# Moving and widening the reduced piece of a streaming grouped convolution: from one piece of 64 columns in slot 23 to pieces of 72 and 4 columns in slot 10

## The chip, the core and the metric

The kernel runs on one core of one Trainium2 chip. The metric is device time in microseconds (us) of one execution. The kernel before has a median of 483.09 us over 4 runs (480.42 to 483.26). One execution was taken with the hardware profiler; it took 481.27 us, and its span, from the first to the last instruction, is 479.5 us.

## What is computed

A grouped convolution with a 1 x 1 window, so nothing but a small matrix product for each pixel and group:

```
H = W = 512;  G = 4;  Cg = 48;  C = 192          # x, out: (1, 512, 512, 192) bf16
out[b, h, w, g, :] = x[b, h, w, g, :] @ w[0, 0, g]    # w: (1, 1, 4, 48, 48)
```

There are 262144 pixels of 192 channels (384 bytes), 100.66 MB in and 100.66 MB out. The arithmetic is small; every byte crosses the DMA engines once in and once out.

## The kernel before

**Tiling.** A "column" is one pixel on each of the 128 partitions, so 128 pixels. A *piece* is a block of columns that one load brings to the ring `ring` and whose result goes out in one or more stores. A *full* piece gives every one of the 128 rows the same number of columns (mostly 80), and its load is a single DMA on SyncE's queue, 128 rows of 80 x 384 = 30720 bytes. The pieces fill numbered *slots* of 80 columns; slot n lies in part n % 3 of the ring (240 columns), and its load waits until TensorE has read slot n - 3 (`freed`, which returns a count of pairs for the semaphore `t_done`).

**The reduced piece.** One piece isn't full. `PARTIAL` lists five blocks of rows, 120 rows in all: rows 16 to 19 and 48 to 51 are left out. Two blocks of 16 rows go by SyncE's queue (loads) and ScalarE's queue (stores), the other three (44, 12 and 32 rows) by GpSimd's. Each block is cut into an outer dimension of units of 4 rows (4, 4, 11, 3 and 8 units), and two tiny "filler" DMAs of 5 rows stand before GpSimd's first and second block. `plan_pieces` (line 73) puts this piece of 64 columns into slot 23; the eight rows left out thus hold 64 columns fewer of the image than the others: 1988 columns against 2052. GpSimd waits for `freed` too, issues its three loads (line 241), waits for `go_sem` from ScalarE, and issues its three stores (line 247).

**Order of pieces.** Slot 0 is split into 8, 24 and 48 columns; slots 1 to 22 are full; 23 is the reduced piece; 24 is full with 80; 25 has the 68 columns that remain. `plan_stores` (line 95) gives each piece one store, except near the end: full pieces with fewer than 240 columns behind them are stored 40 columns at a time, and the last piece, if its size is 68, in parts of 24, 20, 16 and 8 (`LAST_PARTS`). Stores take their place in turn in the output ring `oring` of 280 columns; one that meets the end of the ring is cut in two.

**Compute.** Four columns are a *group* (513 in all), two groups a *pair* (257). For a group TensorE does 6 transposes (line 291) to PSUM; VectorE copies a pair to SBUF (line 349); TensorE does 6 matmuls (line 311) with the block weights; ScalarE copies the group from PSUM to `oring` (line 386), first waiting until the store that last used those columns has landed. ScalarE also issues the stores (line 367), each one group after its last column.

**Program order on TensorE.** `step(pair)` issues the transposes of the next pair and the matmuls of this one. `loop_span` finds the run of full 80-column slots after slot 0, and a loop (`Fori`) of 30 pairs repeats 7 times over slots 1 to 22. Pairs 0 to 9 and the last 37 are written out. In the program there are so 10 + 30 + 37 = 77 pairs of instructions. The other engines' programs are written out in full.

Of the kernel before, what the change touches and what calls it, by code (L numbers as in the profile page):

```python
# [24 lines left out]
BIG = 80  # L25
SLOTS = 3
RCOLS = SLOTS * BIG
# [5 lines left out]
NXP = 4  # L33
NXS = 3
NOB = 4
NTOK = 6
# [3 lines left out]
PARTIAL = (  # L40
    ("sync", 0, 16, 4), ("sync", 32, 16, 4),
    ("pool", 52, 44, 11), ("pool", 20, 12, 3), ("pool", 96, 32, 8),
)
PARTIAL_COLS = 64
PARTIAL_SLOT = 23

FILL_ROWS = 5
FILL_BEFORE = (2, 3)
# [22 lines left out]


def plan_pieces(npix):
    few = PARTIAL_COLS * sum(b[2] for b in PARTIAL)
    partial = npix >= few + 128 * BIG * PARTIAL_SLOT
    cols = (npix - few * partial) // 128
    assert cols % 4 == 0
    head = list(HEAD) if cols >= sum(HEAD) else []
    mid = cols - sum(head)
    slots = [[(BIG, FULL)]] * (mid // BIG) + ([[(mid % BIG, FULL)]] if mid % BIG else [])  # L80
    if head:
        slots.insert(0, [(s, FULL) for s in head])
    if partial:
        slots.insert(PARTIAL_SLOT, [(PARTIAL_COLS, PARTIAL)])
    pieces, g, pix = [], 0, 0
    for n, parts in enumerate(slots):
        c = n % SLOTS * BIG
        for s, blocks in parts:
            pieces.append(Piece(len(pieces), n, c, g, s, blocks, pix))
            c, g, pix = c + s, pieces[-1].g1, pieces[-1].pix_end  # L90
    assert pix == npix
    return pieces
# [21 lines left out]
    return stores  # L114


def loop_span(pieces, ng):

    body = RCOLS // 4
    a = next((p.g0 for p in pieces if p.slot == 1), ng)  # L120
    b = a
    for p in pieces:
        if p.slot >= 1 and p.g0 == b and p.full and p.size == BIG:
            b = p.g1

    rounds = max(0, (b - a - 2) // body)
    return a, body, rounds


def bass_standalone__grouped__vision_kernel(nc, x, w, out):  # L130
# [3 lines left out]
    assert npix % 512 == 0, "the pixel count must be a multiple of 512"  # L134

    pieces = plan_pieces(npix)
    stores = plan_stores(pieces)
    piece_of = {g: p for p in pieces for g in range(p.g0, p.g1)}
    store_of = {g: s for s in stores for g in range(s.g0, s.g1)}
    NG = pieces[-1].g1  # L140
    NP = (NG + 1) // 2
    LA, LB, LR = loop_span(pieces, NG)
    assert LA % 2 == 0 and LB % (2 * NXS) == 0 and LB % (2 * NTOK) == 0 and LB % NXP == 0

    xf = x.rearrange("b h w c -> (b h w) c")
    of = out.rearrange("b h w c -> (b h w) c")
# [2 lines left out]
    def groups(pair):  # L149
        return range(2 * pair, min(2 * pair + 2, NG))  # L150
# [14 lines left out]
    ld_key = {}  # L165
    for p in pieces:
        part = sum(1 for q in pieces if q.slot == p.slot and q.i < p.i)
        for n in range(len(p.blocks)):
            ld_key[p.i, n] = (p.slot % SLOTS, part) if p.full else ("partial", n)
    partial = [p for p in pieces if not p.full]  # L170

    with ExitStack() as es:
        block = es.enter_context(nc.Block())
# [26 lines left out]
        def columns(g):  # L200
            p = piece_of[g]
            at = p.at + 4 * (g - p.g0)
            return ring[:, at * C:(at + 4) * C]
# [6 lines left out]
        def freed(p):  # L210

            last = [q for q in pieces if q.slot == p.slot - SLOTS]
            return last[-1].g1 // 2 if last else 0

        @block.gpsimd
        def _(gp):
# [20 lines left out]
            for p in partial:  # L237
                gp.wait_ge(t_done, freed(p))
                for n, dram, sbuf in transfers(xf, ring, p.at, p, 0, p.size, ("pool",)):
                    filler(n)  # L240
                    gp.dma_start(sbuf, dram).then_inc(ld_sem[ld_key[p.i, n]], 16)  # L241
                gp.wait_ge(go_sem, 1)
                for i, s in enumerate(stores):
                    if s.piece is p:
                        for n, dram, sbuf in transfers(of, oring, s.at, p, s.c0, s.c1, ("pool",)):
                            filler(n)
                            gp.dma_start(dram, sbuf).then_inc(st_sem[i][n], 16)  # L247
# [3 lines left out]
        @block.sync  # L251
        def _(sp):
            sp.dma_start(w_sb[:], wv).then_inc(w_sem, 16)  # L253
            seen = 0
            for p in pieces:
                if freed(p) > seen:
                    seen = freed(p)
                    sp.wait_ge(t_done, seen)
                for n, dram, sbuf in transfers(xf, ring, p.at, p, 0, p.size, ("sync",)):
                    sp.dma_start(sbuf, dram).then_inc(ld_sem[ld_key[p.i, n]], 16)  # L260

        @block.tensor
        def _(pe):

            def build_weights():
                pe.wait_ge(e_sem, 1)
                pe.wait_ge(w_sem, 16)
                last = None
                for (tc, r, g, c0_) in WBLOCKS:
                    s0 = ESHIFT - r  # L270
                    col = WOFF[tc] + c0_
                    last = pe.matmul(o_ps[:, NOB - 1, col:col + CG], lhsT=esel[:, s0:s0 + 128],  # L272
                                     rhs=w_sb[:, g, :], start=True, stop=True, skip_group_check=True)
                last.then_inc(wb_sem, 1)

            def transposes(pair):
                todo = []
                for g in groups(pair):
                    p = piece_of[g]
                    if g % 2 and pair:  # L280
                        pe.wait_ge(e_done[(pair - 1) % NTOK], 1)
                    if g == p.g0:
                        keys = [ld_key[p.i, n] for n in range(len(p.blocks))]
                        for key in keys:
                            pe.wait_ge(ld_sem[key], 16)
                        todo += keys if p.full else []
                    xg = columns(g)
                    for ul in range(2):
                        for tc in range(3):
                            j = ul * 3 + tc  # L290
                            last = pe.transpose(xT_ps[:, g % NXP, j * 128:(j + 1) * 128],  # L291
                                                xg[:, j * 128:(j + 1) * 128], ident[:])
                            if todo and 0 < j < 5:
                                last.then_inc(ld_sem[todo.pop(0)], -16)
                assert not todo
                last.then_inc(t_done, 1)

            def matmuls(pair):
                if pair + 1 == NP or len(groups(pair + 1)) < 2:
                    pe.wait_ge(e_done[pair % NTOK], 1)  # L300
                for g in groups(pair):
                    xs = xT_sb[pair % NXS][:, g % 2 * 2 * UC:(g % 2 + 1) * 2 * UC]
                    if g >= 2:
                        pe.wait_ge(fa_done[(g - 2) % (2 * NTOK)], 1)
                    last = None
                    for ul in range(2):
                        v = 2 * g + ul
                        for tc in range(3):
                            j = ul * 3 + tc
                            c0_, c1_ = COLR[tc]  # L310
                            last = pe.matmul(o_ps[:, v % NOB, c0_:c1_], lhsT=xs[:, j * 128:(j + 1) * 128],  # L311
                                             rhs=wt[:, WOFF[tc]:WOFF[tc] + (c1_ - c0_)],
                                             start=(tc == 0), stop=(tc == 2), skip_group_check=True)
                            if j == 2 and g >= 2:
                                last.then_inc(fa_done[(g - 2) % (2 * NTOK)], -1)
                            if j == 1 and g % 2 == 0:
                                last.then_inc(e_done[pair % NTOK], -1)
                    last.then_inc(mm_done, 1)

            def step(pair):  # L320
                if pair + 1 < NP:
                    transposes(pair + 1)
                matmuls(pair)

            build_weights()
            pe.wait_ge(id_sem, 1)
            transposes(0)
            pe.wait_ge(wc_sem, 1)
            first = LA // 2 if LR > 1 else NP
            for pair in range(first):  # L330
                step(pair)
            if LR > 1:
                with pe.Fori(0, LR):
                    for pair in range(first, first + LB // 2):
                        step(pair)
                for pair in range(first + LR * LB // 2, NP):
                    step(pair)

        @block.vector
        def _(dve):  # L340
# [80 lines left out]
```

## Time and profile before

| what | value |
|---|---|
| median of 4 runs | 483.09 us (480.42 to 483.26) |
| the profiled execution, and its span | 481.27 us, 479.5 us |
| TensorE busy, weight loads busy | 430.9 us (90%), 390.3 us (81%) |
| ScalarE busy | 389.2 us (81%) |
| VectorE busy, GpSimd busy | 246.4 us (51%), 7.0 us (1%) |
| moved by DMA | 201.65 MB, mean 421 GB/s |
| granted TensorE clock | 0.974 |

How to read it: "busy" is the time in which an engine executes; TensorE's matmuls are pipelined, so its busy share isn't a share of its peak. A DMA is cut into packets, one for each row here; 16 DMA engines serve them, each taking one packet at a time from the queues in turn. The trace keeps start, duration, size and queue of every packet, and the time of every semaphore increment; a DMA's semaphore gets its increments as the engines finish their shares, so the sixteen times of one DMA tell how far the engines are apart. Times within the span are counted from its first instruction.

### The profile page before, as it was taken

The page shows a single profiled execution, that of the slowest core. Times are in us where ns is not written, and L with a number is a line of the kernel's source. Part 1 is how long each engine was busy: PE and PEld are TensorE (multiplying, and loading weights), DVE is VectorE, ACT ScalarE, POOL GpSimd, SP SyncE. Part 2 cuts the span into 40 slices and gives each one's busy share as a digit, 9 for nine tenths or more (in the row PEclk, how much of TensorE's full clock was granted, in tenths as well). Part 3 has the DMA queues.
Part 4 walks back from the last instruction along what each step waited for, and adds up shares of the span by engine and source line. Part 5 has one row for each costly group of instructions (what it writes and reads, how often), then busy time and mean ns, then how long its engine had stood idle before and what let it go on. Part 6 is the DMA issues. An engine that isn't in the chain of part 4 may idle for free.

```text
span 479.5 us, 13531 instructions
## 1 busy us (share of the span) xinstructions
PE 430.9 (90%) x6166; PEld 390.3 (81%) x6166; DVE 246.4 (51%) x258; ACT 389.2 (81%) x514; POOL 7.0 (1%) x18
## 2 busy tenths in 40 slices
PE   5999999999979989899899599999898987999894
PEld 4888888988868878788788498988787876888883
DVE  2555655555535545455355345555554543556452
ACT  2899999999958879689689479998797975988895
POOL 1000000000000000000000000000000020000200
PEclk9999999999989999899899889999999998999997
DMA  8999999999999999999999999999999999999986
GB/s 333 430 405 431 437 425 434 424 431 437 431 438 424 441 418 438 425 436 425 419 437 431 439 423 436 425 438 423 431 431 441 428 422 422 404 426 422 430 370 261
DMA packets 9991, 201.65 MB, mean 421 GB/s; under 512 B 1664, under 2 KB 1664, under 8 KB 2432
## 3 DMA queue, kind: packets, MB, share of 16 engines
q10 hardware_dynamic: 5224, 98.50, 48.2%
q1 hardware_dynamic: 4136, 98.52, 48.2%
q0 software_dynamic: 608, 4.33, 2.1%
q8 instruction: 14, 0.23, 0.2%
q14 instruction: 9, 0.07, 0.0%
HBM read 100.68 MB, written 100.66 MB: 420 GB/s over the span
## 4 chain that ended last, share of the span: by engine, by line
PE 46%; DMA 41%; ACT 9%; another core or an unknown queue 1%; issue 1%; ACTq 1%; SPq 0%
DMA out_dram<-oring 39%; PE o_ps L311 27%; PE xT_ps L291 19%; ACT oring L386 9%; DMA ring<-in_x_dram 1%; ACTq L367 1%; SPq L260 0%; SPq L253 0%; ACTq L360 0%; ACTq L369 0%
## 5 line engine op out<-in xcount | busy, mean ns | idle before, releaser
L386 ACT CAST oring<-o_ps 128x768 bf16<-128x768 f32 x513 | 387.9, 801 | 85.2 <-PE o_ps L311 44.1
L349 DVE COPY xT_sb<-xT_ps 128x1536 bf16<-128x1536 bf16 x257 | 245.7, 956 | 222.0 <-PE xT_ps L291 222.0
L311 PE MATMUL o_ps<-wt,xT_sb 128*128 128x144 bf16 (+1 forms) x3078 | 290.1, 237 | 37.2 <-ACT oring L386 33.0
L311 PEld LDWEIGHTS o_ps<-wt,xT_sb 128*128 128x128 bf16 x3078 | 213.7, 99 | 74.6 <-ACT oring L386 66.3
L291 PE MATMUL xT_ps<-ident,ring 128*128 128x128 bf16 x3078 | 222.5, 223 | 3.1 <-DMA ring<-in_x_dram 3.1
L291 PEld LDWEIGHTS xT_ps<-ident,ring 128*128 128x128 bf16 x3078 | 190.2, 100 | 6.1 <-issue 3.5
L234 POOL DMA_DIRECT2D fill<-in_x_dram x4 | 2.4, 598 | 439.4 <-PE xT_ps L291 382.1
L272 PE MATMUL o_ps<-w_sb,esel 48*128 48x48 bf16 x10 | 0.6, 209 | 2.7 <-DMA w_sb<-in_w_dram 2.7
L272 PEld LDWEIGHTS o_ps<-w_sb,esel 48*128 48x128 bf16 x10 | 0.4, 110 | 2.7 <-POOL esel L220 2.7
L342 DVE CAST wt<-o_ps 128x480 bf16<-128x480 f32 x1 | 0.7, 657 | 3.3 <-PE o_ps L272 3.3
L386 ACT ACT_TABLE_LOAD x1 | 1.3, 1283 | 0.8 <-PEq L406 0.8
L241 POOL DMA_DIRECT2D ring<-in_x_dram x3 | 1.7, 564 | 0.0
L247 POOL DMA_DIRECT2D out_dram<-oring x3 | 1.7, 556 | 0.0
L220 POOL TENSOR_SCALAR_AFFINE_SELECT esel<-esel 48x272 bf16<-48x272 bf16 x1 | 0.4, 402 | 0.0
L217 POOL MEMSET esel<- 48x272 bf16 x1 | 0.3, 318 | 0.3 <-POOLq L406 0.3
L224 POOL TENSOR_SCALAR_AFFINE_SELECT ident<-ident 128x128 bf16<-128x128 bf16 x1 | 0.3, 282 | 0.0
L218 POOL MEMSET ident<- 128x128 bf16 x1 | 0.2, 198 | 0.0
L406 POOL MEMSET const-float32-0.0<- 128x1 f32 x1 | 0.1, 98 | 0.3 <-issue 0.3
L406 POOL MEMSET const-bfloat16-1.0<- 128x1 bf16 x1 | 0.1, 102 | 0.0
L406 POOL MEMSET const-uint8-127<- 128x1 uint8 x1 | 0.1, 102 | 0.0
L406 POOL MEMSET const-float32-1.0<- 128x1 f32 x1 | 0.1, 98 | 0.0
## 6 DMA issues: line engine op xcount, KB each, us to landing
ring<-in_x_dram SPq DMA_DIRECT2D x23, 3840.0 KB, 24.7
out_dram<-oring ACTq DMA_DIRECT2D x18, 3840.0 KB, 44.7
out_dram<-oring ACTq DMA_DIRECT2D x9, 1920.0 KB, 41.9
out_dram<-oring ACTq DMA_DIRECT2D x3, 1152.0 KB, 10.7
ring<-in_x_dram SPq DMA_DIRECT2D x1, 3264.0 KB, 25.3
ring<-in_x_dram SPq DMA_DIRECT2D x1, 2304.0 KB, 11.0
out_dram<-oring ACTq DMA_DIRECT2D x1, 2304.0 KB, 27.0
out_dram<-oring ACTq DMA_DIRECT2D x4, 384.0 KB, 9.4
```

The source lines that it names most:

```text
L220: gp.affine_select(out=esel[:], in_=esel[:], pattern=[[-1, ECOLS]], compare_op=AluOpType.is_equal, fill=0.0, base=ESHIFT, channel_multipli ...
L234: gp.dma_start(dst, src).then_inc(fill_sem[k], 16)
L241: gp.dma_start(sbuf, dram).then_inc(ld_sem[ld_key[p.i, n]], 16)
L247: gp.dma_start(dram, sbuf).then_inc(st_sem[i][n], 16)
L272: last = pe.matmul(o_ps[:, NOB - 1, col:col + CG], lhsT=esel[:, s0:s0 + 128], rhs=w_sb[:, g, :], start=True, stop=True, skip_group_check=True)
L291: last = pe.transpose(xT_ps[:, g % NXP, j * 128:(j + 1) * 128], xg[:, j * 128:(j + 1) * 128], ident[:])
L311: last = pe.matmul(o_ps[:, v % NOB, c0_:c1_], lhsT=xs[:, j * 128:(j + 1) * 128], rhs=wt[:, WOFF[tc]:WOFF[tc] + (c1_ - c0_)], start=(tc == ...
L342: dve.tensor_copy(wt[:], o_ps[:, NOB - 1, 0:WCOLS]).then_inc(wc_sem, 1)
L349: dve.tensor_copy(xT_sb[pair % NXS][:, 0:n * 2 * UC].rearrange("p (g c) -> p g c", g=n), xT_ps[:, b0:b0 + n, 0:2 * UC]).then_inc(e_done[pa ...
L367: act.dma_start(dram, sbuf).then_inc(st_sem[i][n], 16)
L386: act.copy(out_columns(g).rearrange("p (u c) -> p u c", u=2), o_ps[:, v % NOB:v % NOB + 2, 0:UC]).then_inc(fa_done[g % (2 * NTOK)] if g < ...
L406: nc = _bacc.Bacc("TRN2", target_bir_lowering=False, num_devices=1)
```

## The change

```diff
-PARTIAL_COLS = 64
-PARTIAL_SLOT = 23
+REST = (("sync", 0, 16, 4),)
+PARTIALS = ((72, PARTIAL), (4, REST))
+PARTIAL_SLOT = 10
...
 def plan_pieces(npix):
-    few = PARTIAL_COLS * sum(b[2] for b in PARTIAL)
+    few = sum(cols * sum(b[2] for b in blocks) for cols, blocks in PARTIALS)
...
-        slots.insert(PARTIAL_SLOT, [(PARTIAL_COLS, PARTIAL)])
+        slots.insert(PARTIAL_SLOT, list(PARTIALS))
...
-def loop_span(pieces, ng):
...
-    rounds = max(0, (b - a - 2) // body)
-    return a, body, rounds
+def loop_spans(pieces):
+
+    body, out, run = RCOLS // 4, [], []
+    for p in pieces + [None]:
+        if p and p.full and p.size == BIG:
+            run.append(p)
+            continue
+        if run:
+
+            first = max((run[0].g0 - 1) // 2, 1)
+            rounds = (run[-1].g1 - 2 * first - 2) // body
+            if rounds > 1:
+                out.append((first, body // 2, rounds))
+        run = []
+    return out
...
-            ld_key[p.i, n] = (p.slot % SLOTS, part) if p.full else ("partial", n)
-    partial = [p for p in pieces if not p.full]
+            ld_key[p.i, n] = (p.slot % SLOTS, part) if p.full else ("partial", part, n)
+    partial = [p for p in pieces if any(b[0] == "pool" for b in p.blocks)]
...
-            return last[-1].g1 // 2 if last else 0
+            return -(-last[-1].g1 // 2) if last else 0
...
-            first = LA // 2 if LR > 1 else NP
-            for pair in range(first):
+            pair = 0
+            for first, body, rounds in LOOPS:
+                for pair in range(pair, first):
+                    step(pair)
+                with pe.Fori(0, rounds):
+                    for pair in range(first, first + body):
+                        step(pair)
+                pair = first + rounds * body
+            for pair in range(pair, NP):
                 step(pair)
```

The reduced piece is 72 columns wide and lies in slot 10. A second piece of 4 columns on rows 0 to 15 alone (`REST`, four units of 4 rows on the SyncE and ScalarE queues) follows it in the same slot, so that the full pieces still have a multiple of 4 columns. Full pieces now hold 1980 columns, so the eight left-out rows hold 1980 columns of the image, rows 0 to 15 hold 1980 + 72 + 4 = 2056 and all other rows 1980 + 72 = 2052. There are 514 groups, still 257 pairs.

What follows in the plan: slots 1 to 9 are full, slot 10 is the reduced one, slots 11 to 24 are full, and slot 25 has 60 columns. As 60 isn't the sum of `LAST_PARTS`, the last piece is stored in parts of 40 and 20. TensorE has two loops: 3 rounds of 30 pairs from pair 9, and 4 rounds of 30 pairs from pair 109; written out are pairs 0 to 8, 99 to 108 and 229 to 256. In the program there are so 9 + 30 + 10 + 30 + 28 = 107 pairs.

More of the change, by code (lines that the diff above doesn't have):

```diff
@@ L114, in plan_stores @@
     return stores
-def loop_span(pieces, ng):
[L119 to L124, printed above, removed]
-    rounds = max(0, (b - a - 2) // body)
-    return a, body, rounds
+def loop_spans(pieces):
[11 more added lines that the diff above has]
+    return out
 def bass_standalone__grouped__vision_kernel(nc, x, w, out):
@@ L141, in bass_standalone__grouped__vision_kernel @@
     NP = (NG + 1) // 2
-    LA, LB, LR = loop_span(pieces, NG)
-    assert LA % 2 == 0 and LB % (2 * NXS) == 0 and LB % (2 * NTOK) == 0 and LB % NXP == 0
+    LOOPS = loop_spans(pieces)
+    assert all(RCOLS // 4 % n == 0 for n in (2 * NXS, 2 * NTOK, NXP))
     xf = x.rearrange("b h w c -> (b h w) c")
@@ L328, in _ @@
             pe.wait_ge(wc_sem, 1)
-            first = LA // 2 if LR > 1 else NP
-            for pair in range(first):
-                step(pair)
[L332 to L337, printed above, removed]
+            pair = 0
[7 more added lines that the diff above has]
+            for pair in range(pair, NP):
+                step(pair)
         @block.vector
```

## The prediction

> **What bounds the kernel now.** I read the slices of the span first, then the table of busy time by stretch, then the waits of a stretch, last the timeline of the end and the trace's packet records.
>
> ```profile
> ACT  2899999999958879689689479998797975988895
> DMA  8999999999999999999999999999999999999986
> ```
>
> ScalarE has holes all through the run, the DMA engines only at both ends. The stretches put numbers to it (columns: length, busy time of the five engines, clock, DMA share, GB/s):
>
> ```profile
> 0.00:5.00 5.00, 0.85 (x14) 0.77 (x15) 0.66 (x1) 1.28 (x1) 1.32 (x8) 1.00 0.55 186
> 5.00:145.00 140.00, 132.41 (x1897) 120.81 (x1896) 75.66 (x79) 117.44 (x156) 0.00 (x0) 0.99 1.01 430
> ...
> 240.00:345.00 105.00, 96.57 (x1396) 87.93 (x1394) 56.40 (x59) 87.38 (x116) 0.00 (x0) 0.97 1.01 433
> ...
> 460.00:479.50 19.50, 12.41 (x174) 10.72 (x174) 6.78 (x8) 12.88 (x17) 0.00 (x0) 0.88 0.72 295
> ```
>
> The share is 1.0 in every long stretch from 5 to 460 us, whatever the engines do. The idle time is at the start (5 x 0.45 = 2.3 us) and at the end (19.5 x 0.28 = 5.5 us). So it is a DMA kernel with a short end in which computing sets the pace for most of the DMA engines. Waits in between matter only through that end. From 240 to 405 us these are ScalarE's:
>
> ```profile
> ACT oring L386 <- DMA out_dram<-oring: 16.4, 5, 5.7
> ACT oring L386 <- PE o_ps L311: 11.2, 41, 1.3
> ```
>
> It waited 16.4 us in 5 waits for stores to land. Yet there was room on average: by the packet records 1593 columns were stored at 400 us and 1720 computed, 127 apart in a ring of 280. The increments of one store's semaphore show why: the store whose landing ended the wait of 401.8 us had its median increment at 385.5, the second-last at 390.5 and the last at 401.8. One engine lags 16 us. From packet to packet on one engine the next starts 4 ns before the last ends, so an engine can be followed: one takes 1.22 us for a store row of 30720 bytes and 1.15 for a load row where the others take 1.138 (+4.4% on both). From 417 to 464 us I can follow it without a gap, and no row of the reduced piece is on it: it is the engine that the piece spares. I call it the slow engine.
>
> The end, with the last two stores:
>
> ```profile
> 473.99 0.34 ACTq L367 DMA_DIRECT2D out_dram<-oring  x1
> 474.37 0.80 ACT L386 CAST oring<-o_ps 128x768 bf16<-128x768 f32 x1 [0.44 <-PE o_ps L311]
> 475.20 0.34 ACTq L367 DMA_DIRECT2D out_dram<-oring  x1
> ```
>
> The last copy ends at 475.2, the span at 479.5, 4.3 us later. For the last store but two (20 columns) the increments have their median at 473.8, the second-last at 474.8, the last at 476.3. Followed back from its last packet (478.7), the last engine has no gap down to 406 us, and it carried rows of the reduced piece, at the nominal 1.138: it isn't the slow engine. The second-last fits the slow one (464.0 plus its 16, 24, 24 and 20 columns). So at the end one ordinary engine is latest, the slow one 1 to 1.5 us before it, and most wait for computing.
>
> **The change part by part.** One column on an engine's 8 rows costs 8 x 1.138/80 = 0.114 us in each direction.
>
> *Columns.* The slow engine loses 8 columns: 8 x 2 x 0.114 x 1.044 = 1.9 us. The ordinary engines had 1988 + 64 and get 1980 + 72: the same 2052. Four of them also get the small piece's units, half an engine's rows: 4 x 2 x 0.057 = 0.46 us. The engine that ends last gets 0 or +0.46.
>
> *Place.* The slow engine's credit (72 columns, 17 us with its slowness) comes at some 150 to 230 us in place of 390 to 460. The store lag (median to last increment) was 10.2 us for the store that landed at 234; it turns into a lead and grows back by the end. ScalarE's waits behind that engine after 240 us (16.4 us) then mostly go. What is late next is the second-slowest (5 us behind at 385 to 390), and then the ring itself: at the first waits, around 140 us, 180 to 195 columns were computed and not stored against 127 later. So computing comes up to 50 columns (some 10 us) nearer to the loads, and I take 5 as what lasts to the end. For the DMA engines the middle is worth 0: they were never idle there.
>
> *Moved issues.* The piece's loads wait for slot 7 in place of slot 20. Before, GpSimd's three landed 16 to 37 us after issue (the last at 423.2), and TensorE began pair 230, which needs them, at 425.2, 40.8 us after the pairs whose end releases them. In the new place the same stretch, pair 80 to 100, runs from 145.9 to 182.5, 36.5 us, so a stall of some 2 us there is possible. Queued behind TensorE's wait are only its own transposes and matmuls, and ScalarE's copies wait for those; the DMA engines go on with stores (175 columns, 20 us, are then computed and not stored). Cost 0; without that cover, 2. The small piece's load adds one more wait to it, on a DMA issued before the next slot's. Rounding `freed` up delays the later slots' loads by one group's copy (0.8 us); they land 24.7 us after issue, with two slots of computing (33 us) in hand: 0. ScalarE's issues of the two four-unit blocks took 2.0 us at 441.9 and 1.8 us more went by before its next copy; this stood in the computing of the end and now stands in the middle, with a third block; there the same 20 us of stores cover it. TensorE lost 2.0 us there (a pair of 3.61 in place of 1.6): gain for the end of computing, 2.
>
> *TensorE's loops.* Back edges and exits show no gap: pairs 40, 70, 100 and 220 take 1.5 to 1.7 us like the rest. Written-out code is fetched:
>
> ```profile
> q8 instruction: 14, 0.23, 0.2%
> ```
>
> Fourteen packets of 16384 bytes for 77 pairs, 0.95 us each; 107 pairs make 20. Six more are 5.7 us over 16 engines, mean 0.4 (consecutive ones weren't on one engine); between 0 and 1 for the engine that ends last; I take the mean.
>
> *The end.* Group 514 adds one copy (0.80) and makes the last pair whole (VectorE 0.96 against 0.56): +1.2 us for computing. The last stores are 40 and 20 columns against 24, 20, 16 and 8. If computing sets the end: the 40 are issued four copies before the last copy's end (3.3 us), their data starts 1.4 us after issue (as at 473.99) and takes 4.6, the 20 another 2.3; with 0.9 to the span's end this is 5.8 us behind the last copy in place of 4.3. If the DMA queue sets it, coarse stores cost nothing.
>
> **The sum.** Computing: 475.2 + 1.2 - 2.0 - 5 = 469.4, and 5.8 later 475.2. The ordinary engine that ends last: 479.5 + 0.4 for fetches, less what its luck changes. It lost 2.9 us after 405 in five long packets (one of 2.16 us in place of 1.14, a fetch and its follower); with the middle place another engine may be last. Between nothing and the 2.5 us that lie between last and median increment, I take the half, 1.25; the small piece counts with 4 engines in 15, 0.1: 479.5 + 0.4 + 0.1 - 1.25 = 478.7. The later of the two sums counts: the DMA engines. The profiled execution had 1.8 us around its span (481.27) and lies 0.4% under the median, so I scale: 483.09 x 478.7/479.5 = **482.3**, a gain of 0.2%. Its own range is 477.4 (479.5 + 0.4 - 2.5) to 481.0 (a whole fetch and the small piece on the last engine), on the median's scale 481.0 to 484.6.
>
> *A rule against the change.* The slow engine took 1.22 us for a store row and carries no row of the reduced piece. The Trainium skill (DMA: Bandwidth & Descriptors, "Latency and other measured facts") says that engines 7 and 15 are usually the slower ones, its cause being uncertain, and the page's "The descriptor swizzle" gives the spared rows 16 to 19 and 48 to 51 to engine 4. By the rule the spared engine would be a wrong one and its 1.9 us worth 0; no record here numbers the engines, but the chain of packets shows the slow one spared, and the sum goes by the chain.
>
> **The rivals.**
>
> *The whole end closes (faster).* Computing is 5 us or more earlier and no engine is far behind: then the 5.5 us of mean idle time at the end fall to about 2.3 (0.9 from the last landing to the span's end and 1.4 of spread), with 0.4 more for fetches: 479.5 - 3.2 + 0.4 = 476.7, 480.3 on the median's scale; with all but the 0.9 gone and one cheap fetch, 475, 478.6. For it: ScalarE's 16.4 us. Against: the last engine had no gap to close.
>
> *Computing sets the end (slower).* One mechanism, in the last 60 columns: ScalarE's waits stay, because the ring of 280 columns or the second-slowest engine takes over from the slow one, and the two coarse stores lie bare behind a longer chain. Last copy at 475.2 + 1.2 = 476.4 with the 2 us lost again at late store waits, end 482.2, 485.8 on the median's scale. It decides when the last copy is later than 478.7 - 5.8 = 472.9. For it: the chain of waits is TensorE and ScalarE from 402 us on; the parts 24, 20, 16 and 8 no longer fit.
>
> *It relieves what isn't the limit.* The slow engine wasn't last, so sparing it more and earlier changes ScalarE's waits and not the time: 479.5 + 0.4 = 479.9, 483.5. That lies in the forecast's own range and is counted with it.
>
> **How the numbers follow.** A measurement of this kernel tells about 0.5% from no change (480.7 to 485.5). Forecast with the last rival 0.49, the faster 0.29, the slower 0.22; the chances are these. The forecast of 482.3 is the likeliest case. The range goes down to the faster rival's floor (478.6) less a little for luck in packets, 478.0, and up past the slower one with a fetch and a stall on the last engine (482.2 + 1 = 483.2, 486.8): 487.0.
>
> **What would show it.** Right: DMA share 1.0 from 5 us to 465 or later; 20 packets of instructions; from 240 us on, ScalarE's waits for stores well under 16 us and the last increment of each store within some 5 us of the median; the last copy before 473. The slower rival: last copy after 474 and a gap of about 6 us behind it. The faster one: mean idle time at the end under 3 us. Wrong altogether: stalls of TensorE on `ring` around 185 us that reach the end, or holes in the DMA row in the middle.

## The result, and the profile after

The changed kernel takes 482.94 us in the median (480.44 to 490.28, 42 runs), the kernel before on the same chip 482.35 us (63 runs). The ratio is 1.0033, with a 95% interval of 1.0018 to 1.0049: a loss of a third of a per cent, inside the range of the prediction and on the other side of no change than its forecast. Some executions of either kernel take over 1.5% longer than its fastest; the ratio leaves them out and the medians don't, so the ratio isn't the quotient of the two medians (1.0012). The profiled execution of the changed kernel took 484.69 us with a span of 482.9 us; it lies 1.75 us above the median of its kernel, so its last microseconds have to be read with care.

First the page of the changed kernel: ScalarE's and the DMA engines' slices, and the queue of instruction packets (packets, MB, share of 16 engines).

```profile
ACT  2999999999959971979973899888988877888880
DMA  8999999999999999999999999999999999999994
...
q8 instruction: 20, 0.33, 0.2%
```

The 20 packets are there. The DMA row has no hole in the middle, as in the kernel before; its last digit fell from 6 to 4. So more of the engines are idle at the end, not fewer. The timeline of the end shows that computing isn't why:

```profile
467.93 0.34 ACTq L373 DMA_DIRECT2D out_dram<-oring  x1
...
468.31 3.06 ACT L392 CAST oring<-o_ps 128x768 bf16<-128x768 f32 x4 [0.44 <-PE o_ps L316]
...
471.40 0.34 ACTq L373 DMA_DIRECT2D out_dram<-oring  x1
```

The last copy ends at 471.4, 3.8 us earlier than before (475.2). But the span ends 11.5 us behind it in place of 4.3. The last store's increments tell who is late: median 476.5, second-last 480.8, last 482.4 (before: 478.1, 478.2, 479.0). Most engines finished 1.6 us earlier than before and two finished 1.8 and 3.4 us later than the last one before.

ScalarE's waits for stores between 240 and 405 us, and the stand of TensorE behind the piece's loads:

```profile
ACT oring L392 <- DMA out_dram<-oring: 10.0, 2, 7.7
```

```profile
176.95 1.06 PE L316 MATMUL o_ps<-wt,xT_sb 128*128 128x144 bf16 x12
187.84 1.44 PE L296 MATMUL xT_ps<-ident,ring 128*128 128x128 bf16 x12 [9.84 <-DMA ring<-in_x_dram]
```

16.4 us in five waits became 10.0 in two, one of them 7.7. And TensorE stood 9.84 us before pair 100, the first that reads the reduced piece: GpSimd's three loads were issued from 145 us on and landed at 162.7, 178.6 and 187.7. This is the stall "around 185 us" that the prediction named as a sign of being wrong altogether; whether it reaches the end is asked below.

Last the view that points at the cause. The columns are those of the table by stretch: length, busy time of the five engines, clock, DMA share, GB/s.

```profile
200.00:220.20 20.20, 18.23 (x272) 16.45 (x268) 10.81 (x12) 16.95 (x23) 2.76 (x5) 1.00 1.00 428
220.20:224.40 4.20, 4.14 (x63) 3.74 (x62) 2.60 (x3) 3.87 (x7) 0.00 (x0) 1.00 0.91 388
224.40:240.00 15.60, 15.37 (x230) 13.85 (x228) 8.72 (x10) 14.09 (x20) 0.00 (x0) 1.00 1.03 438
```

In 4.2 us the share falls to 0.91 and the rate to 388 GB/s, while every computing engine is busy. In the kernel before the same stretch shows 1.03. The column is inexact in so short a stretch, so I counted packets: from 220.2 to 224.5 us exactly 15 of the 16 engines had one, and from 282.6 to 284.4 us again. One engine in sixteen makes 0.06 in a share and nothing in the tenths of the page. Followed from packet to packet, the idle one is the slow engine, the very one that the reduced piece is there to spare. SyncE's issue times say why it stood: it issued its next loads at 223.2 and at 283.3, and the two stretches end 1.4 and 1.1 us later with packets of these loads. So the engine had nothing else queued.

### The profile page after: what moved, and what is told of

It reads as the page before. It is cut to its first block, busy times and chain, and to the rows that moved or that the text cites. A ratio compares the mean times of both kernels' runs of the same rounds, so it can differ in the third digit from the quotient of the medians.

```text
span 482.9 us, 13571 instructions
## 1 busy us (share of the span) xinstructions
PE 430.0 (89%) x6178; PEld 388.4 (80%) x6178; DVE 246.8 (51%) x258; ACT 388.6 (80%) x515; POOL 7.0 (1%) x18
## 4 chain that ended last, share of the span: by engine, by line
PE 48%; DMA 38%; ACT 8%; ACTq 1%; issue 1%; POOL 1%; SPq 0%
DMA out_dram<-oring 28%; PE o_ps L316 28%; PE xT_ps L296 20%; DMA ring<-in_x_dram 10%; ACT oring L392 8%; ACTq L373 1%; POOL fill L239 0%; POOL ring L246 0%; POOL out_dram L252 0%; SPq L265 0%; SPq L258 0%; ACTq L366 0%; ACTq L375 0%
## 5 line engine op out<-in xcount | busy, mean ns | idle before, releaser
L296 PE MATMUL xT_ps<-ident,ring 128*128 128x128 bf16 x3084 | 221.5, 222 | 12.8 <-DMA ring<-in_x_dram 12.8
```

## The experiments

All ratios are to the kernel before on the same chip, with 95% intervals. Four theories were written down at first: **M**, the piece in the middle costs (GpSimd's loads come late there and the DMA engines lose time); **E**, the coarse last stores; **F**, the six more instruction packets, each of which lies on one engine; **C**, the prediction's own, that stores cover what happens in the middle. **I**, the idle slow engine, came only when M had been narrowed down, and was written down before the last two runs. In the code cuts below, `...` stands for what is left out.

### The parts of the change alone

Place alone: one piece of 64 columns as before, without the small piece and with the old last parts, in slot 10.

```diff
-PARTIALS = ((72, PARTIAL), (4, REST))
+PARTIALS = ((64, PARTIAL),)
```

> The place alone: the reduced piece keeps its 64 columns and moves from slot 23 to slot 10; the last piece keeps 68 columns and its fine parts; two TensorE loops, 107 pairs written out. Theory M (the middle costs: GpSimd's loads come some 10 us after TensorE wants them, computing stands, and the DMA packets of that stage get longer, by some 1 us per engine): as slow as the whole change, ratio 1.002 to 1.005, with TensorE waiting 5 to 10 us on the ring near 180 us. Theory E (the coarse last stores of 40 and 20 cost): 0.998 to 1.001. Theory F (six more packets of instructions cost, each on one engine): 1.001 to 1.004, as under M, with no wait needed.

Measured: 1.0035 (1.0000 to 1.0071). In its trace (488.74 us, where the median is 483.54) the last copy ends at 480.6 and the median increment of the last store is at 483.5, so there most engines were late, not one alone. Size alone, with the place of before:

```diff
-PARTIAL_SLOT = 10
+PARTIAL_SLOT = 23
```

> The size alone: 72 and 4 columns in slot 23 as before, the last piece 60 in parts of 40 and 20, one TensorE loop and 76 pairs written out. Theory M: 0.998 to 1.001 (no stall in the middle, the slow engine relieved by 1.9 us). Theory E: 1.002 to 1.005. Theory F: 0.999 to 1.001.

Measured: 1.0053 (1.0011 to 1.0095). The last copy of this kernel ends at 480.1, 4.9 us later than before, and the span 5.4 us behind it. And the changed kernel with finer last parts:

```diff
-LAST_PARTS = (24, 20, 16, 8)
+LAST_PARTS = (24, 16, 12, 8)
```

> The whole change, but the last piece of 60 columns goes out in parts of 24, 16, 12 and 8 in place of 40 and 20. Theory M: still 1.002 to 1.005, the last engine in the records still 4 us or more behind the median one. Theory E: 0.999 to 1.001. Theory F: 1.001 to 1.004.

Measured: 1.0050 (1.0022 to 1.0079). Each part alone costs about as much as both together, as far as the intervals tell, so they don't add up. Fine parts gain nothing in slot 10. **E falls** for the changed kernel, whose last copy isn't what the end waits for.

The same fine parts in the old slot, run later, complete the square (both edits above, on the changed kernel):

> The widths of after (72 and 4 columns) in the old slot 23, with the last 60 columns stored as 24, 16, 12 and 8. Size alone gave 1.0053, with last parts of 40 and 20 behind a last copy at 480.1. If the coarse parts cost what the prediction gave them (5.8 us behind the last copy in place of 4.3): 0.3% less, 1.001 to 1.003. If sparing the slow engine 8 more columns is worth its 1.9 us in the old place as well: 0.998. If neither counts: 1.004 to 1.006.

Measured: 1.0062 (1.0028 to 1.0097). The span ends 3.1 us behind the last copy, against 5.4 with the coarse parts, 2.3 us less in these two traces; the prediction had 1.5 (5.8 against 4.3). But the last copy came at 482.5 here, so nothing was gained. In this trace TensorE stood 7.06 us behind the wider piece's loads late in the run:

```profile
429.35 1.44 PE L296 MATMUL xT_ps<-ident,ring 128*128 128x128 bf16 x12 [7.06 <-DMA ring<-in_x_dram]
```

In the trace with coarse parts this stand is 1.00 us, and its last copy is late too, at 480.1. Here the DMA engines ran dry near the end, which the changed kernel's did not (first the row of the kernel with fine parts in slot 23, then that of the changed kernel):

```profile
440.00:460.00 20.00, 17.92 (x266) 16.09 (x263) 10.53 (x11) 16.34 (x22) 2.75 (x5) 1.00 0.78 327
440.00:460.00 20.00, 19.07 (x279) 16.91 (x277) 11.47 (x12) 16.92 (x24) 0.00 (x0) 1.00 0.99 418
```

Counted by packets, some ten of the sixteen engines were idle on average from 446.8 to 453.7 us in the first, and 3.6 from 447.6 to 451.3 us in the kernel with coarse parts in slot 23; in the kernel before all sixteen had packets throughout this time, and in none of the three was the slow engine idle before 440 us. That both kernels with the wide piece in slot 23 lose time there and end behind a late last copy is shown; by which wait it comes isn't.

### The instruction packets

30 pairs more written out in the kernel before, 107 in place of 77:

```diff
-    rounds = max(0, (b - a - 2) // body)
+    rounds = max(0, (b - a - 2) // body - 1)
```

> The kernel before with 6 rounds of its loop in place of 7, so that 107 pairs are written out in place of 77: 20 packets of instructions in place of 14, nothing else changed. Theory M and theory E: 0.999 to 1.001. Theory F: 1.001 to 1.004, mean +0.4 us per engine and up to 2 us if the engine that ends last takes two of them.

Measured: 1.0047 (1.0013 to 1.0081). Beside it the kernel before itself, as a measure of chance:

> The kernel before itself, sent as an experiment, to see what the comparison gives for no change at all. All theories: 0.998 to 1.002. A value like those of the first four runs (1.0035 to 1.0053) would say that they can't be told from no change.

Measured: 1.0020 (0.9988 to 1.0053). The first seemed to speak for F, but the second shows that 0.2% can come from nothing. So I took the dose up: no loop at all, 257 pairs.

```diff
-    rounds = max(0, (b - a - 2) // body)
+    rounds = 0
```

> The kernel before with TensorE's program written out whole: no loop, 257 pairs of instructions in place of 77. About 47 packets of instructions in place of 14 (14 for 77 pairs, 20 for 107). Fetches on single engines (F): in the traces so far the packets go in turn to 8 of the 16 DMA engines, 0.95 us each, with about 0.4 us more on the packet behind; 47 packets are 6 on each of the eight where 14 are at most 2, so the last engine gets 4 x 1.35 = 5.4 us more, of which up to 3 us vanish in the engines' idle time at the end: ratio 1.005 to 1.011. As the prediction had it (a mean over 16 engines): 33 x 0.95 / 16 = 2.0 us, hidden in the idle time at the end or not: 1.000 to 1.004.

```profile
q8 instruction: 48, 0.79, 0.6%
```

Measured: 1.0037 (1.0001 to 1.0073). 34 more packets cost no more than six seemed to. The interval still reaches into F's range (1.005 to 1.011). But even its upper end, 0.73% for 34 packets, makes 0.13% for six if packets cost in proportion, less than half of the loss: **F falls as the main cause**. The 1.0047 of the run with six more stays unexplained; chance of the size that the kernel beside itself shows may be part of it. What F said of the engines is true. Followed to the end, the 48 packets lie on eight engines, six on each, none on the other eight; those eight end at 479.8 to 481.8 us, the other eight, the slow one among them, all at 477.1 to 477.2. Six packets, 5.7 us at 0.95 each, thus set an engine back by 2.7 to 4.7 us behind engines that wait for computing anyway. By the measured ratio, six packets in all are worth some 0.07%, an estimate (6/34 of 0.37%).

### A stall by itself, and no reduced piece

The kernel before, in which ScalarE makes the copy of group 200 thirteen times; each new copy waits for the one before:

```diff
+STALL_GROUP = 200
+STALL_COPIES = 12
...
+                if g == STALL_GROUP:
+                    for k in range(STALL_COPIES):
+                        act.copy(out_columns(g)..., o_ps[...]).then_inc(stall_sem, 1)
+                        act.wait_ge(stall_sem, k + 1)
```

> The kernel before with computing held up once in the middle: ScalarE makes the copy of group 200 thirteen times in place of once, each waiting for the one before, some 10 to 12 us at 180 us. Nothing else changes, the DMA engines get no more bytes. Theory M (a stall of computing leaves the load queue dry, loads and stores then go in step and their packets get longer): 1.002 to 1.005, long packets in the 60 us behind the stall. Theory C (the prediction's cover: 20 us of stores in hand make a stall of 10 us free): 0.999 to 1.001.

Measured: 1.0025 (0.9980 to 1.0069). Unclear by itself: it allows nothing and it allows 0.7%. Its trace has no stretch from 40 to 440 us in which an engine was idle for long (under 1 us in any 20 us, added over all sixteen), so a stall of computing in the middle needn't stop the DMA engines: in this trace C holds.

The kernel before without any reduced piece:

```diff
-    partial = npix >= few + 128 * BIG * PARTIAL_SLOT
+    partial = False
```

> The kernel before without a reduced piece: all 128 rows hold 2048 columns, GpSimd moves nothing, the last piece has 48 columns in parts of 40 and 8. The slow engine then has 60 columns more than in the kernel before (14.3 us with its slowness), the others 4 fewer (0.9). If the slow engine bounds the end without the piece: its lag of 1 to 1.5 us before the last one grows by 15, ratio 1.02 to 1.03. If its lag doesn't matter, as the forecast's rival had it: 0.998 to 1.002.

Measured: 1.0198 (1.0145 to 1.0251), last increment at 488.0, second-last at 485.0. Leaving the piece out costs 2% in all. In its trace most engines end later too (the median increment is at 484.9, against 478.1 before), and the edit also changes the last parts and frees GpSimd, so the 2% aren't the slow engine's own rows alone. The rule of the Trainium skill that stood against the change (DMA: Bandwidth & Descriptors, "Latency and other measured facts", engines 7 and 15 as the slower ones) doesn't fit this run, if the piece's rows map to engines as that page has it: the spared engine is the one that needs it.

### Holding SyncE back

The changed kernel, in which SyncE waits until GpSimd's three loads have landed before it loads the piece behind; that load goes out at 177 us in place of 161.

```diff
+                if p.i and pieces[p.i - 1].slot == PARTIAL_SLOT and p.full:
+                    for q in partial:
+                        for n, bl in enumerate(q.blocks):
+                            if bl[0] == "pool":
+                                sp.wait_ge(ld_sem[ld_key[q.i, n]], 16)
```

> The whole change, but SyncE issues the load behind the reduced piece only when GpSimd's three loads have landed, so that these share the engines with the stores alone. GpSimd's loads should land some 15 us earlier and TensorE's wait of 9.8 us for the ring at 178 us go or fall under 3. Theory M: 0.999 to 1.002. Theory F (packets of instructions): still 1.002 to 1.005.

Measured: 0.9978 (0.9945 to 1.0010). A second and a third time, the third beside the changed kernel on one chip:

> The held kernel once more (after, in which SyncE waits for GpSimd's three loads before it loads the piece behind). If its 0.998 was more than chance: 0.996 to 1.000, that is 0.3 to 0.5% below after's 1.003. If it was chance: 1.002 to 1.005. F alone expects the latter, as it has 20 packets of instructions like after.

> The held kernel for the third time, beside the changed kernel on the same chip: 0.996 to 1.000 if GpSimd's loads against SyncE's next load are what costs the time; 1.002 to 1.005 if the hold does nothing.

> The changed kernel itself once more, beside the held one on the same chip. Fetches on single engines and the place cost what the first measurement showed: 1.002 to 1.005, and the held kernel 0.3 to 0.6% below it. If the difference between the two was one of chips or of chance: the two within 0.2%.

Measured: 0.9988 (0.9962 to 1.0013) and 0.9991 (0.9966 to 1.0016); the changed kernel itself 1.0041 (1.0016 to 1.0065). The hold is worth half a per cent, and not by sparing TensorE its stand: TensorE waits 14.5, 14.5 and 11.2 us for loads in the three held traces, 12.8 and 11.0 in the two of the changed kernel. So the stall of 9.84 us doesn't have to reach the end. Is it the pause in the loads as such? The same pause at slot 15, far from GpSimd's loads:

```diff
-                if freed(p) > seen:
-                    seen = freed(p)
+                need = freed(p)
+                if p.slot == 15 and p.full:
+                    need += 10
+                if need > seen:
+                    seen = need
```

> The changed kernel with the same pause in SyncE's loads in another place, where GpSimd has no loads: the load of slot 15 waits ten pairs longer and goes out together with that of slot 16. If any pause of one slot in the loads gains (the engines draw level while the load queue is empty): 0.996 to 1.000, as the held kernel. If it is GpSimd's loads that need the room: 1.002 to 1.006, as the changed kernel or worse.

Measured: 1.0060 (1.0023 to 1.0096). No: a pause elsewhere makes it worse. In its trace SyncE's loads stop from 220.2 to 261.7 us, and from 241.6 us on at least one engine has no packet for 7.8 us.

### The place

The two pieces in slot 4, without and with the hold:

```diff
-PARTIAL_SLOT = 10
+PARTIAL_SLOT = 4
```

> The kernel after with its two pieces in slot 4 in place of 10. The first run of full slots is then too short for a loop and the second takes 6 rounds: 77 pairs written out and 14 packets of instructions, as before the change, with the widths of after and an early place. F (the six extra packets cost the time): 0.997 to 1.001 of the kernel before. M (the place away from the end costs the time, by GpSimd's late loads and by engines that drift apart): 1.003 to 1.005, as after. The prediction's reasons without the fetch: 0.998.

> Both: the pieces of after in slot 4 (14 packets of instructions) and SyncE's wait for GpSimd's three loads. If fetches and late loads each cost 0.3%: 0.994 to 0.997, the fastest of all. F alone: as the kernel with slot 4, 0.997 to 1.001. If neither counts: 1.002 to 1.005.

Measured: 1.0109 (1.0067 to 1.0151) and 1.0044 (1.0013 to 1.0075). My expectation had the number of packets wrong: one loop of 6 rounds leaves 77 pairs outside it, and its body of 30 pairs is written once as well, so 107 pairs and 20 packets, as after. These two runs thus say nothing on F; they tell of the place alone. The place costs, and slot 4 costs more than slot 10, as M in general has it. The table by stretch of slot 4 without the hold:

```profile
98.10:100.70 2.60, 2.57 (x40) 2.27 (x38) 1.85 (x2) 2.33 (x4) 0.00 (x0) 1.00 0.95 402
100.70:111.00 10.30, 8.40 (x129) 7.62 (x127) 4.86 (x6) 7.83 (x12) 2.76 (x5) 1.00 1.04 437
111.00:118.80 7.80, 7.71 (x116) 6.91 (x114) 4.68 (x5) 7.21 (x11) 0.00 (x0) 1.00 0.93 396
```

Two dips again, of 2.6 and 7.9 us, with the computing engines busy in both. 0.93 and 0.95 are close to fifteen sixteenths (0.94). Both end about 1 us after SyncE's next load, issued at 99.8 and 117.9. This is where theory I came from. The slow engine takes some 4% longer for every row, so it falls behind by a few hundredths of the time that has passed. The piece gives it 72 columns' worth, 17 us, at once. Early in the run it isn't 17 us behind; it gets ahead of the others, comes to the end of what is queued for it, and stands. What it loses there it can't make up, so the theory goes, and it is late at the end. Later in the run it is further behind, the credit fills a debt, and nothing is lost. If so, the idle time should vanish at a later slot, and the hold should have nothing to gain there:

```diff
-PARTIAL_SLOT = 10
+PARTIAL_SLOT = 16
```

> The changed kernel with both pieces in slot 16 in place of 10 (two loops, 107 pairs, 20 packets of instructions as after). Idle slow engine (I): the engine that the piece spares is 8 to 10 us behind at slot 16 in place of some 6 at slot 10, so its credit of 17 us makes a lead of 6 to 8 us in place of 10 to 11, and of that it stood idle 3 to 6 us at slot 10 (8 to 10 us at slot 4, nothing at slot 23); at slot 16 at most 2 us are left, it ends with the others, and the time is 0.996 to 1.000 of the kernel before. Late loads of GpSimd against SyncE's next load (M): the same at any slot, 1.002 to 1.005.

> The same with SyncE's wait for GpSimd's three loads. I: what the hold gained at slots 10 and 4 it gained by shortening or moving the slow engine's idle time, so here it gains nothing more: within 0.2% of the kernel without it. M: 0.3 to 0.6% below the kernel without it, at 0.997 to 1.000.

Measured: 0.9985 (0.9959 to 1.0011) and 0.9985 (0.9956 to 1.0014). Both are what theory I expects, and neither is what M as a fixed price of GpSimd's late loads expects. Two other things differ at slot 16. TensorE waits less for loads there (7.4 us in all), but the held kernels in slot 10 wait up to 14.5 without a loss. And the ring `oring` cuts the last stores in other places, but slot 4 has the same cuts there and was the slowest. ScalarE waited 18.6 us in all for stores at slot 16, more than the 13.8 of the changed kernel, and its last copy ended at 471.8, no earlier; so what was gained wasn't gained in computing.

The traces side by side. "Idle" is the time from 40 to 440 us in which the slow engine, followed from packet to packet, had no packet, in stretches of over 0.1 us; where the end says "not followed", it is the time in which one engine had none. The next two columns are the ends of the last packets. The held kernel in slot 16 has no row: its trace is of an execution of 489.75 us, where the median is 481.82.

| kernel, slot | idle of the slow engine | slow engine ends | last other engine ends | ratio |
|---|---|---|---|---|
| before, 23 | 0 | 477.7 | 478.7 | 1 |
| changed, 10 | 4.3 at 220 and 1.8 at 283 | 480.8 (second-last increment) | 482.4 (last increment) | 1.0033 |
| changed, second trace | 2.3 at 222 and 2.0 at 283 | 481.0 | 478.8 | 1.0041 |
| held, 10 | 3.6 at 222 | 477.9 | 477.7 | 0.9978 |
| held, second trace | 5.9 at 223 | 481.4 | 479.9 | 0.9988 |
| held, third trace | 2.3 at 220 | 474.9 | 477.2 | 0.9991 |
| place alone, 10 | 4.6 at 239 (and some engine 2.3 at 411) | 483.2 | 486.2 | 1.0035 |
| changed with fine parts, 10 | 1.5 at 221 (and 2.5 engines on average for 2.6 at 284) | not followed; increments 482.0, 483.1 | | 1.0050 |
| pause at slot 15, 10 | 1.4 at 220 and 7.8 at 242 | not followed | | 1.0060 |
| slot 4 | 2.6 at 98 and 7.9 at 111 | not followed; increments 481.1, 485.5 | | 1.0109 |
| slot 4, held | 2.4 at 60 and 2.3 at 110 | 477.5 | 481.3 | 1.0044 |
| slot 16 | 0 | 477.9 | 479.3 | 0.9985 |

The first idle stretch in each of the held traces, in the place-alone kernel and in the second trace of the changed kernel ends, like those above, about 1 us after SyncE's next load (224.5, 228.0, 221.4, 242.1 and 223.0): what is shown is that the slow engine had run out of work each time.

In the trace of slot 16 the end is denser than that of the changed kernel (0.70 over its last 22.9 us):

```profile
460.00:480.10 20.10, 9.99 (x138) 8.46 (x138) 5.27 (x6) 10.48 (x14) 0.00 (x0) 0.84 0.79 329
```

What stays open in part is the hold. It takes away the second idle stretch (at 283 us, 2 us, in both traces of the changed kernel and in none of the three held ones), and with it ScalarE's long wait that came before it, which was 7.74 us in the first trace of the changed kernel and 9.46 in the second:

```profile
261.22 0.80 ACT L392 CAST oring<-o_ps 128x768 bf16<-128x768 f32 x1 [9.46 <-DMA out_dram<-oring]
```

In the held kernel's third trace the only such wait between 240 and 300 us is this, and the other two have none:

```profile
251.08 0.80 ACT L397 CAST oring<-o_ps 128x768 bf16<-128x768 f32 x1 [0.89 <-DMA out_dram<-oring]
```

SyncE's loads show the step between. In the two traces of the changed kernel they come at 239.9, 266.6 and 283.3, and at 239.7, 267.3 and 284.0, the second some 27 us behind the first; in the held traces they come every 17 us there. So loads were short when the slow engine ran out at 283 us. Two microseconds are 0.4% of the time and would do, but the first idle stretch varies from 2.3 to 5.9 us between traces of one kernel (the trace with 5.9 was of the longest of 12 runs, 484.19 us where the median was 480.99), so the link from the second stretch to the half per cent is argued, not shown. Nor does idle time alone order the ratios: slot 4 with the hold has 4.7 us of it at 1.0044, the second held trace 5.9 at 0.9988. That the hold gains nothing at slot 16 speaks for the link.

## Why the prediction was wrong, step by step

**What bounds the kernel: right, but read too coarsely.** It is a DMA kernel with a short end. "The DMA engines only at both ends" have holes, I said, from a share that is a mean over sixteen engines. For the kernel before this was true for each one of them.

**Columns: not tested alone.** The slow engine's 1.9 us stand in the sum below; no run isolates them, and size alone in slot 23 lost time for another reason.

**Place: the step that failed.** I wrote "For the DMA engines the middle is worth 0: they were never idle there." I had the lag (10.2 us for a store at 234) and the credit (17 us) beside each other, and I said that the lag "turns into a lead". I didn't ask how far an engine can lead. The sum for the slow engine would have been: 477.7 (its last packet before), less 1.9 for the columns, plus the idle time, 4.3 to 6.1 us, so 480.1 to 481.9. The traces have 481.0 and, as second-last increment, 480.8. With the 0.9 us from its last packet to the end of the span (481.0 to 481.9 in the second trace) that is a span of 481.0 to 482.8; the median of the changed kernel less the 1.8 us around its span (484.69 less 482.9) is 481.1. The same sum misses other traces by 2 to 3 us: 475.8 for slot 16, where the trace has 477.9, and 478.1 for the third held one, where it has 474.9. So it gives the size of the loss and not its last microsecond. I left that engine out of the sum because it was 1 to 1.5 us before the last one.

**Luck: the wrong sign, and no cause.** I took off 1.25 us for the ordinary engine that ended last. Without this term the sum is 479.5 + 0.4 + 0.1 = 480.0, or 483.6 on the median's scale, 0.1% above the kernel before: the gain that I forecast came from luck alone. In the profiled execution of the changed kernel another ordinary engine was last: it lost 9.1 us in long packets (the others, bar the slow one, 2.4 to 5.4) and ended 1.6 us behind the slow one. In the second trace none did. This may be why the profile lies above its median; as the second trace has the loss without it, it isn't the loss.

**Moved issues: cost sized wrong, cover right.** I priced TensorE's stand at "some 2 us"; it was 9.84, since GpSimd's last load took 41 us from 146.8 to 187.7. Yet TensorE stands as long in the held kernel, which is no slower than before. The cover of stores held for the other engines, bar stretches of under 1 us near 272 and 288; it didn't hold for the slow one.

**Computing: right.** Forecast for the last copy was 469.4, measured 471.4 and, in the second trace, 468.2; the condition "before 473" is met, ScalarE's waits fell from 16.4 to 10.0. So these traces gained 3.8 to 7 us in computing against the one of before (a second trace of the kernel before, the one beside itself, has its last copy at 477.7), and the DMA engines didn't let them through: the faster rival lost its price where the slow engine lost its credit. The slower rival (computing sets the end) didn't occur.

**Instruction packets: 0.4 us was a fair price, for a wrong reason.** They aren't spread over 16 engines but lie on eight; the run with 34 more makes six of them worth 0.3 us by its ratio and 0.6 us by the upper end of its interval, both estimates in proportion.

Of the signs that I named, "the last increment of each store within some 5 us of the median" was the one that failed: 5.9 and 6.4 us at the last store, and 8 to 11 us for most stores between 300 and 440 us in the first trace. In the second trace the last increment at the end was the slow engine's.

## What to carry to other kernels

A busy share over many servers hides one that is idle: where the work was balanced by hand for one slow server, count the time in which all but one have work. Credit for a slow server is worth only as much as it is behind when it gets it, unless more work is queued for it, and the rest runs out as idle time. Giving it later helped here (slot 16 against 10 and 4), though the wide piece very late, in slot 23, lost time in another way; giving it in small portions wasn't tried. And a gain in computing counts only as far as the last server of the next stage isn't made later by the same edit.

Of the kernels here, the one with slot 16, with the hold or without, and the held one with slot 10 are the best: all some 0.5% faster than the changed kernel, and none told apart from the kernel before by its interval.

## What the runs showed of the hardware

- Instruction packets (16384 bytes, 0.95 us each) go in turn to eight of the sixteen DMA engines: in the kernel without a loop the packets at 18, 89, 166, 248, 326 and 403 us lie on one engine, those at 29, 98, 175, 256, 334 and 418 on the next. The other eight got none in that run.
- Runs of one kernel differ by more than the effect in question: half of the 63 runs of the kernel before lie between 480.8 and 484.5 us, and its own copy measured 1.0020. A single trace can't carry a third of a per cent.
- Packets take longer in some stretches: in the place-alone kernel those of 400 to 420 us took 24 us longer, over the 16 engines, than at 1.138 us for 30720 bytes, in the kernel before 15, and in that of slot 16 1.4. The same rise stands at the start of every trace (22 to 28 us up to 40 us). What causes it isn't shown.
- A load issued by SyncE reaches an engine that has no other work about 1 us later: the idle stretches of the slow engine at slot 10 end 0.9 to 1.4 us after the next load's issue.
